# Turning a block's sums: f32 matmuls with the identity instead of f32 transposes

## Chip, cores, metric

The kernel runs on one core of one Trainium2 chip. The metric is the device time of one execution in microseconds (us). TensorE (PE) multiplies, VectorE (DVE), ScalarE (ACT) and GpSimd (POOL) do the elementwise work, and SyncE (SP) issues most of the transfers.

## The reference

The kernel computes the output and the seven gradients of a transformer-like block: attention with 32 heads of 16 columns on a layer-normed input, multiplied by a SiLU gate that an MLP makes of the same input.

```
S, D, H, DH, F = 2048, 512, 32, 16, 1792        # rows, columns, heads, columns of a head, MLP width

xn  = layernorm(x)
s   = attention(xn) @ wo                         # softmax(q k^T / 4) v, per head
g   = silu(gelu(layernorm(xn) @ w1 + b1) @ w2 + b2)
out = x + s * g

out, vjp = jax.vjp(f, x, wqkv, wo, w1, b1, w2, b2)
return out, *vjp(grad_out)
```

All inputs and outputs are bf16. The work that matters here is the core of the attention, which runs the forward and the backward pass together.

## The kernel before

The program has three stages: projections, layer norms and the MLP's first half (`phase_pre`), the attention's core (`attention_core`), and the weights' and the input's gradients (`phase3`). The change lies in the core.

The core works through 64 blocks. Block `j` is a pair of heads (16 pairs) and a quarter of the queries (4 quarters of 512). In a block it goes over 16 groups of 128 keys, `g = 16 j + kb`, for both heads `hj`:

- `s` (line 1532): scores, keys by queries, on PE. `S` (line 1546): their exponential `et`, on ACT.
- `a1` (line 1555): PE multiplies [v, 1, k] by `et` and adds it into rows 0 to 63 of the PSUM bank `X`. After 16 groups these rows hold the block's sums: for each head 16 value sums and the softmax sum (the rest of its 32 rows isn't used).
- `d` (line 1628): PE multiplies the other half of the keys' operand by the tile `dt`. `m` (line 1632): DVE multiplies `d` by `et` into `gts`.
- `a2` (line 1561): PE adds into rows 64 to 127 of `X`; these become the gradient of q. The copy out of it is `dq` (line 1643), on ACT.
- `t` (line 1542) and its exponential (line 1550) make scores the other way round, queries by keys. For two units of a block PE turns `et` instead (`E`, line 1570) and DVE copies the result (`eE`, line 1574). `ze` and `zg` (lines 1663 and 1671) add up the keys' gradients in a bank `Z`; the operand `gk` of `zg` is `gts`, turned by a transfer that SP issues (line 1635). `acc` (lines 1685 and 1687) copies or adds `Z` on DVE.

When a block's 16 groups are in `X`, its sums must be turned, so that queries lie on partitions. This is the chain of the block's end, and the place of the change:

- `xs` (line 1587): DVE copies rows 0 to 63 of `X` to SBUF, 64 x 512, f32.
- `XT` (line 1593): PE turns it in four pieces of 64 x 128 into one PSUM bank, 128 x 4 x 64, f32.
- `xt` (line 1597): DVE copies that bank. `rL` (line 1601): DVE takes the reciprocals of the softmax sums.
- `W` (lines 1610 to 1613): POOL makes the normalized output and the operand `W`.
- `DT` (line 1618) and `dt` (line 1622): PE turns `W`, DVE copies it; `dt` is what the block's `d` matmuls stream.

The tiles `XT`, `DT`, `ET` and `Z` share one PSUM bank (tag `z`), so each waits for the copy of the one before. `d` has one bank for each head, and the scores share two slots of two banks.

The order on every engine is written out ahead: `make_plan` goes through estimated costs, due times (`due`) and free buffers, and `attention_core` emits the steps in that order under a manual schedule. In the estimate `XT` has an entry of its own (line 1199: 400 ns for the group, then a gap of 205). The lag between steps is part of the plan: while one block's sums are turned, PE already works at the scores of the next block and the `d` of this one's predecessor. Matmuls of zeros into `X` (`fill`, lines 1578 and 1580) stand where the plan leaves PE a gap.

One other f32 matmul appears in the argument. Line 451, in `phase_pre`, spreads the heads' largest key norms over all partitions: `ones_h`, 32 x 128, times a diagonal, 32 x 32, both f32.

Of the kernel before, what the change touches and what calls it, by code (L numbers as in the profile page):

```python
# [1452 lines left out]
def attention_core(ctx, tc, opnds, ps_z, tail, NAT_s, NATQ_s, Oall, dQall, dKVT_out, dQT_out, ident_f32, ident_bf, npairs=16, nqc=4):  # L1453

    nc = tc.nc
# [133 lines left out]
    def emit_XT(j):  # L1589
        xs = tiles.pop(("xs", j))  # L1590
        XT = tiles["XT", j] = ps_z.tile([128, 4, 64], f32, name="XT", tag="z")
        for qb in range(4):
            nc.tensor.transpose(XT[:, qb, :], xs[:, qb * 128:(qb + 1) * 128], ident_f32[0:64, 0:64])

    def emit_xt(j):
        xt = tiles["xt", j] = finp.tile([128, 4, 64], f32, name="xt")
# [94 lines left out]
    def emit_sk(p, hj):  # L1691
        ob = tiles["ob", p]
        for x in range(2):
            r0 = p * 64 + hj * 32 + 16 * x
            nc.gpsimd.dma_start(out=dKVT_out[r0:r0 + 16, :], in_=ob[64 * x + 32 * hj:64 * x + 32 * hj + 16, :])

    ET_ = mybir.EngineType
    f = dict(fill=emit_fill, E=emit_E, eE=emit_eE, s=emit_s, t=emit_t, S=emit_exp_s, T=emit_exp_t, a1=emit_a1, a2=emit_a2, xs=emit_xs, XT=emit_XT, xt=emit_xt, rl=emit_rl,
             W=emit_W, DT=emit_DT, dt=emit_dt, d0=lambda g: emit_d(g, 0), d1=lambda g: emit_d(g, 1), m0=lambda g: emit_m(g, 0),
             m1=lambda g: emit_m(g, 1), ze=emit_ze, zg=emit_zg, acc=emit_acc, dq=emit_dq,  # L1700
# [127 lines left out]
```

## Time and profile before

| what | us |
|---|---|
| median of 3 runs | 2188.24 |
| the three runs | 2188.24, 2172.43, 2189.15 |
| the profiled execution | 2197.41 |
| its span, first to last instruction | 2195.6 |

The span is what the trace covers; the profiled execution's own time holds 1.8 us more around it. Its mean granted TensorE clock was 0.976. In the rows of the profile PE stands for matmuls, PEld for loads of the stationary operand (they overlap with PE), and L12 for line 12 of the kernel. A tile's rows are written `out<-in`, with buffer numbers left out; `x4` behind a row of the timeline means that four instructions were merged, and the time in brackets is the engine's idle time before them, with what ended it.

### The profile page before, as it was taken

The page shows a single profiled execution, that of the slowest core. Times are in us where ns is not written, and L with a number is a line of the kernel's source. Part 1 is how long each engine was busy: PE and PEld are TensorE (multiplying, and loading weights), DVE is VectorE, ACT ScalarE, POOL GpSimd, SP SyncE. Part 2 cuts the span into 40 slices and gives each one's busy share as a digit, 9 for nine tenths or more (in the row PEclk, how much of TensorE's full clock was granted, in tenths as well). Part 3 has the DMA queues.
Part 4 walks back from the last instruction along what each step waited for, and adds up shares of the span by engine and source line. Part 5 has one row for each costly group of instructions (what it writes and reads, how often), then busy time and mean ns, then how long its engine had stood idle before and what let it go on. Part 6 is the DMA issues. An engine that isn't in the chain of part 4 may idle for free.

```text
span 2195.6 us, 46078 instructions
## 1 busy us (share of the span) xinstructions
PE 2092.3 (95%) x17683; PEld 749.9 (34%) x17683; DVE 1954.9 (89%) x3485; ACT 1894.6 (86%) x2194; POOL 349.9 (16%) x672
## 2 busy tenths in 40 slices
PE   7999999999999999999999999999999999889999
PEld 3443332333333323323333333233323333334444
DVE  7675999999999999989999999999989997889355
ACT  6667999999999999989999999999989994776233
POOL 4322011111110111111111111120111011520001
PEclk9999999999999999989999999999989998999999
DMA  9884999999999999999999999999999999994971
GB/s 288 273 276 135 226 221 216 228 232 233 226 224 234 222 219 232 230 214 215 234 227 225 229 233 210 229 232 236 227 202 236 221 219 229 264 240 112 181 236 60
DMA packets 1562958, 484.49 MB, mean 221 GB/s; under 512 B 1532432, under 2 KB 1536784, under 8 KB 1562096
## 3 DMA queue, kind: packets, MB, share of 16 engines
q1 hardware_dynamic: 1546256, 441.56, 101.0%
q0 software_dynamic: 12560, 34.74, 6.1%
q10 hardware_dynamic: 3920, 5.24, 0.7%
q8 instruction: 138, 2.26, 0.4%
q14 instruction: 84, 0.69, 0.1%
HBM read 46.52 MB, written 51.12 MB: 44 GB/s over the span
## 4 chain that ended last, share of the span: by engine, by line
PE 64%; DVE 16%; ACT 8%; DMA 7%; issue 3%; SPq 1%; POOL 1%; DVEq 0%; ACTq 0%; POOLq 0%
PE d L1628 13%; PE Z L1663 10%; PE X L1555 9%; DVE gts L1632 8%; PE s L1532 8%; PE t L1542 5%; DMA gk<-gts 4%; ACT e L1550 3%; PE ps_dy L853 2%; PE ps_dhg L787 2%; DVE xs L1587 2%; PE ps_dw L729 2%; DVE eE L1574 2%; ACT et L1546 1%; PE ps_dw L771 1%
## 5 line engine op out<-in xcount | busy, mean ns | idle before, releaser
L1632 DVE TENSOR_TENSOR gts<-d,et 128x512 bf16<-128x512 f32 x1424 | 904.4, 682 | 38.4 <-PE d L1628 19.4
L1546 ACT ACTIVATE et<-s 128x1024 bf16<-128x1024 f32 x712 | 721.6, 1066 | 26.4 <-PE d L1628 15.7
L1628 PE MATMUL d<-dt,KVT 32*128 32x512 bf16 x2048 | 720.7, 388 | 18.3 <-DVE gts L1632 6.4
L1550 ACT ACTIVATE e<-t 128x1024 bf16<-128x1024 f32 x640 | 671.6, 1072 | 29.5 <-PE d L1628 14.8
L1532 PE MATMUL s<-QDT,KVT 32*128 32x512 bf16 x2048 | 403.8, 386 | 23.5 <-ACT e L1550 9.1
L1632 DVE TENSOR_TENSOR gts<-d,dQall 128x512 bf16<-128x512 f32 x624 | 396.7, 682 | 18.3 <-PE d L1628 7.9
L1561 PE MATMUL X<-gts,NAT 128*32 128x512 bf16 x2048 | 407.7, 395 | 0.0
L1671 PE MATMUL Z<-gk,QW 128*32 128x512 bf16 x2048 | 386.1, 396 | 15.8 <-DMA gk<-gts 15.8
L1546 ACT ACTIVATE dQall<-s 128x1024 bf16<-128x1024 f32 x312 | 315.8, 1070 | 11.1 <-PE d L1628 10.1
L1555 PE MATMUL X<-et,NAT 128*32 128x512 bf16 x1424 | 281.4, 392 | 0.8 <-ACT et L1546 0.8
L1542 PE MATMUL t<-KVT,QDT 32*128 32x512 bf16 x1280 | 256.6, 390 | 0.0
L1628 PEld LDWEIGHTS <-KVT 32*128 32x128 bf16 x2048 | 169.1, 91 | 226.8 <-issue 221.7
L1663 PE MATMUL Z<-e,W 128*32 128x512 bf16 x1280 | 243.8, 393 | 0.3 <-DVE xt L1597 0.2
L1532 PEld LDWEIGHTS <-KVT 32*128 32x128 bf16 x2048 | 135.3, 91 | 243.1 <-issue 215.2
L1663 PEld LDWEIGHTS <-W 128*32 128x32 bf16 x2048 | 105.7, 93 | 245.4 <-issue 244.0
L1610 POOL TENSOR_TENSOR On<-xt,rL 128x128 f32<-128x128 f32 x64 | 25.4, 396 | 993.4 <-DVE rL L1601 993.4
L1555 PEld LDWEIGHTS <-NAT 128*32 128x32 bf16 x2048 | 103.0, 95 | 127.1 <-issue 126.9
L1542 PEld LDWEIGHTS <-QDT 32*128 32x128 bf16 x1280 | 82.6, 91 | 140.7 <-issue 128.0
L1555 PE MATMUL X<-dQall,NAT 128*32 128x512 bf16 x624 | 123.6, 392 | 0.0
L1561 PEld LDWEIGHTS <-NAT 128*32 128x32 bf16 x2048 | 100.6, 95 | 63.7 <-issue 57.2
L1663 PE MATMUL Z<-gk,W 128*32 128x512 bf16 x512 | 102.9, 397 | 0.0
L1671 PEld LDWEIGHTS <-QW 128*32 128x32 bf16 x2048 | 89.2, 94 | 25.1 <-DMA gk<-gts 15.5
(223 smaller groups left out, 2621.6 us busy)
## 6 DMA issues: line engine op xcount, KB each, us to landing
gk<-gts SPq DMA_TRANSPOSE x512, 4.5
H1T_s<-h1p SPq DMA_DIRECT2D x28, 256.0 KB, 4.0
dQall<-H1T_s POOLq DMA_DIRECT2D x28, 256.0 KB, 5.0
HGT_s<-hgT SPq DMA_DIRECT2D x21, 256.0 KB, 3.8
NAT_s<-NS SPq DMA_DIRECT2D x4, 1056.0 KB, 5.3
dKVT_s<-ob POOLq DMA_DIRECT2D x64, 64.0 KB, 3.9
gb<-GB_s SPq DMA_DIRECT2D x8, 512.0 KB, 5.9
Rkv<-dKVT_s SPq DMA_DIRECT2D x2, 2048.0 KB, 10.4
```

Of the source, the lines that this page charges most:

```text
L729: nc.tensor.matmul(ps[:], lhsT=hgc[fc // 2][:, t // 4, fc % 2, t % 4, :], rhs=dm_all[:, t, :], start=(t == 0), stop=(t == NT - 1))
L787: nc.tensor.matmul(ps[:], lhsT=w2T[:, dc, fc * 128:(fc + 1) * 128], rhs=dmT[:, dc, ss], start=(dc == 0), stop=(dc == IC - 1))
L1532: nc.tensor.matmul(s[:, hj, :], lhsT=op["KVT"][r, kb * 128:(kb + 1) * 128], rhs=op["QDT"][r, qc * 512:(qc + 1) * 512], start=True, stop=Tr ...
L1542: nc.tensor.matmul(t[:, hj, :], lhsT=op["QDT"][r, q0:q0 + 128], rhs=op["KVT"][r, kc * 512:(kc + 1) * 512], start=True, stop=True, tile_pos ...
L1546: nc.scalar.activation(out=et_of(g)[:, g % 2], in_=tiles.pop(("s", g))[:], func=ACT.Exp)
L1550: nc.scalar.activation(out=e[:], in_=tiles.pop(("t", u))[:], func=ACT.Exp)
L1555: nc.tensor.matmul(X[32 * hj:32 * hj + 32, :], lhsT=op_of(j)["NAT"][:, kb, hj, 0:32], rhs=et_of(g)[:, g % 2, hj], start=(kb == 0), stop=(k ...
L1561: nc.tensor.matmul(X[64 + 32 * hj:96 + 32 * hj, :], lhsT=op_of(j)["NAT"][:, kb, hj, 1:33], rhs=gts_of(g // 2)[:, g % 2, hj], start=(kb == ...
L1628: nc.tensor.matmul(d[:], lhsT=op_of(j)["KVT"][r, kb * 128:(kb + 1) * 128], rhs=tiles["dt", j][r, :], start=True, stop=True, tile_position= ...
L1632: nc.vector.tensor_tensor(out=gts_of(g // 2)[:, g % 2, hj], in0=tiles.pop(("d", g, hj))[:], in1=et_of(g)[:, g % 2, hj], op=ALU.mult)
L1663: nc.tensor.matmul(cur["Z"][32 * hj:32 * hj + 32, :], lhsT=tiles["W", j][:, qb, hj, :], rhs=rhs_of(tiles["e", j, kc], hj, qb) if e is None ...
L1671: nc.tensor.matmul(cur["Z"][64 + 32 * hj:96 + 32 * hj, :], lhsT=QW[p % 2][:, qc * 4 + qb, hj, :], rhs=rhs_of(tiles["g", j, kc], hj, qb), s ...
```

## The change

The four f32 transposes of a block's sums become four matmuls with `xs` as the stationary and the identity as the moving operand. The operands, their shapes, the output and the place in the order are the same.

```
     def emit_XT(j):
         xs = tiles.pop(("xs", j))
         XT = tiles["XT", j] = ps_z.tile([128, 4, 64], f32, name="XT", tag="z")
         for qb in range(4):
-            nc.tensor.transpose(XT[:, qb, :], xs[:, qb * 128:(qb + 1) * 128], ident_f32[0:64, 0:64])
+            nc.tensor.matmul(XT[:, qb, :], lhsT=xs[:, qb * 128:(qb + 1) * 128], rhs=ident_f32[0:64, 0:64], start=True, stop=True)
```

In the built program the two instructions differ in one flag (transpose or not); all five engines issue the same instructions in the same order as before.

More of the change, by code (lines that the diff above doesn't have):

```diff
@@ L1592, in emit_XT @@
         for qb in range(4):
-            nc.tensor.transpose(XT[:, qb, :], xs[:, qb * 128:(qb + 1) * 128], ident_f32[0:64, 0:64])
+            nc.tensor.matmul(XT[:, qb, :], lhsT=xs[:, qb * 128:(qb + 1) * 128], rhs=ident_f32[0:64, 0:64], start=True, stop=True)
     def emit_xt(j):
```

## The prediction

> **What bounds the kernel now.** I read the page's head and its chain first, then the windows of single blocks, then the rows around one turning of the sums, and last the one place where this kernel already does an f32 matmul that is no transpose.
>
> ```profile
> span 2195.6 us, 46078 instructions
> PE 2092.3 (95%) x17683; PEld 749.9 (34%) x17683; DVE 1954.9 (89%) x3485; ACT 1894.6 (86%) x2194; POOL 349.9 (16%) x672
> PE 64%; DVE 16%; ACT 8%; DMA 7%; issue 3%; SPq 1%; POOL 1%; DVEq 0%; ACTq 0%; POOLq 0%
> ```
>
> Three engines are busy for most of the span and the chain changes between them, so shares alone decide nothing. The instructions that change are these (the view of tile XT: count, then min/median/max in ns, first and last start in us; below it, who ended PE's wait before them, us and times):
>
> ```profile
> L1593 PEld LDWEIGHTS XT<-ident_f,xs x256: 133/138/141, 201.3 to 1807.3; 64*128 64x128 f32 x128
> L1593 PE MATMUL XT<-ident_f,xs x256: 221/223/275, 201.3 to 1807.3; 64*128 64x64 f32 x128
>   DVE eE L1574: 17.6, 67
> ```
>
> There are 64 blocks with four transposes each, from 201.3 to 1807.3 us. That is 1606.0 us for 63 steps, 25.49 us each. Four single steps, in the windows view (us; then busy time of PE, PEld, DVE, ACT, POOL; then the granted clock, DMA share, GB/s):
>
> ```profile
> 1018.96:1043.92 24.96, 24.27 (x241) 8.12 (x240) 24.68 (x43) 24.74 (x28) 5.76 (x11) 1.00 1.06 218
> 1143.78:1168.74 24.96, 24.29 (x241) 8.11 (x240) 24.68 (x43) 24.74 (x28) 2.44 (x6) 1.00 1.22 224
> 960.56:993.62 33.06, 29.64 (x241) 8.18 (x240) 25.67 (x43) 25.64 (x28) 3.60 (x8) 0.74 1.18 203
> 1600.15:1631.89 31.74, 29.67 (x241) 8.19 (x240) 25.70 (x43) 25.64 (x28) 2.16 (x5) 0.73 1.26 225
> ```
>
> An undisturbed step takes 24.96 us, twice to the hundredth: a cycle with no loose place, in which DVE is idle for 0.28 us and ACT for 0.22. Disturbed steps make up the rest: 1606.0 - 63 x 24.96 = 33.5 us. In the two that are shown, PE had a quarter less than its full clock. So the question is whether the turning lies on that cycle. One block's rows (start, duration, engine):
>
> ```profile
> 1018.15 2.86 ACT L1546 ACTIVATE et<-s 128x1024 bf16<-128x1024 f32 x3
> 1018.20 0.67 DVE L1574 COPY eE<-ET 128x1024 bf16<-128x1024 bf16 x1
> 1018.80 1.27 DVE L1632 TENSOR_TENSOR gts<-d,et 128x512 bf16<-128x512 f32 x2
> 1018.95 0.32 PEld L1593 LDWEIGHTS XT<-ident_f,xs 64*128 64x128 f32 x4 [0.23 <-DVE eE L1574]
> 1018.96 0.46 PE L1593 MATMUL XT<-ident_f,xs 64*128 64x64 f32 x4
> 1019.34 0.09 PEld L1628 LDWEIGHTS <-KVT 32*128 32x128 bf16 x1
> 1019.53 0.37 PE L1628 MATMUL d<-dt,KVT 32*128 32x512 bf16 x1
> 1019.53 0.39 PE L1532 MATMUL s<-QDT,KVT 32*128 32x512 bf16 x2
> 1020.00 0.40 DVE L1597 COPY xt<-XT 128x256 f32<-128x256 f32 x1
> 1020.33 0.67 DVE L1632 TENSOR_TENSOR gts<-d,et 128x512 bf16<-128x512 f32 x1
> ```
>
> The eE copy ends at 1018.20 + 0.67 = 1018.87 and frees the PSUM bank. XT starts 0.09 later, d and s follow 0.57 after XT's start. The d matmul waits for something else: the first of the two gts products ends at 1018.80 + 0.67 = 1019.47 and d starts 0.06 later. The chain of waits, one block on, goes through the same place:
>
> ```profile
> 1043.24 0.60 DVE eE L1574
> 1043.84 0.61 DVE gts L1632
> 1044.44 0.04 issue
> 1044.49 0.37 PE d L1628
> 1044.86 0.02 PE s L1532 x2
> 1044.88 0.32 PE X L1555 x2
> ...
> 1048.52 0.02 PE d L1628
> 1048.54 0.67 DVE acc L1685
> ```
>
> The rows left out are PE's, without a break. So eE starts both branches: gts and then d, which is on the chain, and XT and then d, which is not. The second is nearly as long. How nearly is told by a block in which XT came late:
>
> ```profile
> 993.62 0.46 PE L1593 MATMUL XT<-ident_f,xs 64*128 64x64 f32 x4
> 994.01 0.09 PEld L1628 LDWEIGHTS <-KVT 32*128 32x128 bf16 x1
> 994.08 0.37 PE L1628 MATMUL d<-dt,KVT 32*128 32x512 bf16 x1
> ```
>
> Here d starts 0.46 us after XT's start. So the four transposes have 0.57 - 0.46 = 0.11 us to spare in an ordinary block, and whatever they take beyond that moves d, and with it the s matmuls and all that PE issues after them.
>
> **The change part by part.** It swaps 256 f32 transposes for 256 f32 matmuls of the same operands (xs stationary, the identity moving). Nothing is reordered, no wait is added or taken away, no tile changes, the plan's own estimate of the step stays. The consumers (xt, rL, the POOL products, DT) are the same. What is open is the price of the instruction, and the kernel has it once: line 451 multiplies f32 ones by an f32 diagonal, in one call. Line 451 in the source view, then in the timeline with the weight load that follows:
>
> ```profile
> L451 PEld LDWEIGHTS ps_kb<-kmd,ones_h x2: 181/182/184, 75.0 to 75.1; 32*128 32x128 f32 x2
> L451 PE MATMUL ps_kb<-kmd,ones_h x2: 271/282/293, 75.0 to 75.1; 32*128 32x32 f32 x2
> 75.00 0.29 PEld L451 LDWEIGHTS ps_kb<-kmd,ones_h 32*128 32x128 f32 x2 [0.42 <-issue]
> 75.00 0.40 PE L451 MATMUL ps_kb<-kmd,ones_h 32*128 32x32 f32 x2
> 75.33 0.76 PEld L269 LDWEIGHTS <-w_sb 128*128 128x128 bf16 x5
> ```
>
> One call left two weight loads and two matmuls, where a transpose leaves one pair (256 of each for 64 x 4). I therefore expect 512 pairs at line 1593, eight per block. The distance between loads, with 128 columns loaded in both cases: for the transposes (0.32 - 0.14) / 3 = 0.06 us; at line 451, 0.29 - 0.18 = 0.11 us. The next load follows 75.33 - 75.11 = 0.22 after line 451's last one, and 1019.34 - 1019.13 = 0.21 after the transposes' last.
>
> The first d after the new group then can start, counted from the first load, after 7 x 0.11 + 0.22 + 0.07 = 1.06 us (0.07 from d's load to d, in the block with the late XT). Today it starts at 0.57. So d is late by 0.49 us per block. The bounds of the distance: not below 0.06, the transposes' own, which gives 7 x 0.06 + 0.29 = 0.71 and 0.14 us per block; 0.13 by the matmuls of line 451 instead of its loads (0.40 less 0.27 for one of them), 1.20 and 0.63 us; and 0.18, one load's whole duration, if nothing overlaps, 1.55 and 0.98 us. I take 0.11, since the row is of the same load, and line 451 streams 32 columns where XT streams 64, which could only push it up. A gain from the instruction itself is excluded: each has the same operands, and no row of an f32 matmul is shorter than the transposes.
>
> [...] The row: twice the pairs, 0.11 / 0.06 = 1.8 times as far apart, 3.7 times together. [...]
>
> What hides it? XT's consumers first. XT now ends at 1018.96 + 0.46 = 1019.42 and xt starts at 1020.00, so 0.58 us of its growth is covered; the new end, about 7 x 0.11 + 0.05 + 0.28 = 1.10 after the start, or 1020.06, costs the copy some 0.1 us. For the d branch there is no cover but the 0.11 us already counted. The d that is 0.49 later ends at 1019.90 + 0.49 = 1020.39, and the gts that takes it started at 1020.33, so DVE goes idle. The s beside it, ready at 1019.53 + 0.39 = 1019.92, feeds the third of the three activations that run back to back from 1018.15 to 1021.01, so ACT goes idle too. Both have only the 0.28 and 0.22 us per step that they idle today, and these lie at other places.
>
> The sum: 63 steps x 0.49 = 31 us. Against the profiled execution, 2197.4 us (its span 2195.6 and 1.8 us around it), that makes 2228 us. The median of the runs shown is 2188.2, so there 2219 us, 1.4% more. With the bounds: 63 x 0.14 = 9 us, 63 x 0.63 = 40 us, 63 x 0.98 = 62 us.
>
> **The rivals.** *The pairs cost more.* The distance is 0.13 or above, since 64 columns are streamed instead of 32, or a load has to wait for the matmul before it. For it: both durations at line 451 are longer than the transposes' (182 against 138 ns, 282 against 223). Against it: the second load there began 0.11 after the first, before the first matmul's 0.28 were over. 2188 + 40 = 2228 to 2250. Chance 0.20.
>
> *Slack elsewhere takes half of it.* The late d is made up for later in the step, at a place where PE waits for ACT or DVE. For it: DVE and ACT are 24.7 of 24.96 busy, not all of it. Against it: the chain after d runs PE row after PE row for the next 4 us. 2188 + 15 = 2203. Chance 0.11.
>
> *The change doesn't do what it says*: the identity matmul is built as one pair, or as two at the old distance. Then d is late by at most 0.14 us, 2188 to 2197. Line 451's two records speak against it. Chance 0.06.
>
> *Not slower, by the transfers.* The 33.5 us of disturbed steps begin where Z waits for a gk that a transfer has to turn:
>
> ```profile
> PE Z L1671 <- DMA gk<-gts: 14.2, 10, 2.9
> PEld L1671 <- DMA gk<-gts: 13.3, 9, 3.3
> ```
>
> These are the two rows of that wait in the view of waits over 201 to 1807 us: some ten times, up to 3.3 us. In the two steps shown the granted clock was 0.74 and 0.73, so a wait of 3 us costs 7 to 8 in all. A step that is 2% longer gives the same ten turnings 2% more time; if SP's queue then catches up, the waits and the slow stretches go. The point at which it decides: all 31 us of the sum have to be found in the 33.5, that is, nearly every disturbed step must vanish, 2186 us; 9 us found is enough for a result within 1%. Against it: the turnings start from products that are late by the same 0.49 us, and the quiet steps have no wait to lose. Chance 0.11, of it 0.03 that it comes together with cheap pairs, 2188 + 9 - 33 = 2164.
>
> **How the numbers follow.** About 1%, 22 us, is what a measurement of this kernel can tell from no change: 2166 to 2210. My forecast has the chance 0.52: 2219 us, by itself 2210 to 2230. Slower by over 1%: 0.52 + 0.20 = 0.72. Within 1%: 0.11 + 0.06 + 0.08 = 0.25. Faster: 0.03. The range goes down to 2196, where the half-absorbed case and the upper part of the cheap pairs are still held, and up to 2240, into the dearer pairs; outside are the 0.11 of the transfers, some 0.02 of the cheap pairs and 0.05 above.
>
> **What would show it.** In the profile after: 512 loads and 512 matmuls at line 1593, and 256 more PE instructions on the page; loads 0.11 apart (a group of about 0.95 us instead of 0.32); the first d 1.06 us after the group's start, no longer released by gts; quiet steps of 25.45 us instead of 24.96, clock 1.00. The prediction is wrong if the loads stay 256, if quiet steps stay under 25.2 us with eight pairs in them, or if the disturbed steps change by more than 10 us.

## The result and the profile after

| what | before | after |
|---|---|---|
| median of 21 runs each, us | 2178.2 (2170.74 to 2189.15) | 2193.59 (2186.67 to 2210.14) |
| ratio, 95% interval | | 1.0066 [1.0051, 1.0082] |
| the profiled execution, us | 2197.41 | 2186.67 |
| its span, us | 2195.6 | 2184.9 |

The kernel became slower by 15.4 us, 0.7%: within the 1% that the prediction took for no change, though the interval is clear of 1. The two profiled executions stand the other way round. The one of before is slower than any of these 21, the one of after is as fast as the fastest of its own. So the two traces may be compared step by step, but not by their totals.

The head of the page of after, the granted clock in 40 slices of the span, and the chain of waits by engine:

```profile
span 2184.9 us, 46546 instructions
PE 2095.1 (96%) x17895; PEld 787.0 (36%) x17939; DVE 1962.8 (90%) x3485; ACT 1891.0 (87%) x2194; POOL 349.1 (16%) x672
PEclk9999999999999999999999999999999998999999
PE 53%; ACT 24%; DVE 13%; issue 6%; DMA 3%; POOL 1%; SPq 0%; DVEq 0%; ACTq 0%; POOLq 0%
```

PEld has exactly 256 instructions more than before (17939 - 17683); PE has 212 more on record, since some matmul records are missing. The clock row of before is:

```profile
PEclk9999999999999999989999999999989998999999
```

Slices 18 and 30, in the core, are under nine tenths there and full now. The 8 in slice 34 is in both; that slice begins behind the core's last block.

The turning in the view of tile XT (count, then min/median/max in ns, first and last start in us), and the copy that precedes it, 64 times, in the view of tile xs:

```profile
L1593 PEld LDWEIGHTS XT<-ident_f,xs x512: 182/188/188, 201.7 to 1802.8; 64*128 64x128 f32 x171
L1593 PE MATMUL XT<-ident_f,xs x512: 272/272/320, 201.7 to 1802.8; 64*128 64x64 f32 x171
L1587 DVE COPY xs<-X x64: 670/672/683, 200.0 to 1800.6; 64x512 f32<-64x512 f32 x64
```

512 pairs, as forecast. The 63 steps of the core, taken from the first xs to the last, last 1600.6 us, against 1606.0 before. Two single steps in the windows view (us; busy time of PE, PEld, DVE, ACT, POOL; granted clock; DMA share; GB/s):

```profile
962.36:987.79 25.43, 24.71 (x245) 8.68 (x243) 24.86 (x43) 24.75 (x28) 3.62 (x8) 1.00 1.22 228
1573.05:1598.48 25.43, 24.71 (x246) 8.68 (x244) 24.86 (x43) 24.75 (x28) 3.61 (x8) 1.00 1.22 228
```

The undisturbed step went from 24.96 to 25.43 us. Over 63 steps that is 29.4 us (with the medians of the trace unrounded, 0.466 us each). But in this trace nearly every step is such a step (the longest takes 26.23 us): 1600.6 - 63 x 25.43 = -1.5 us, where 33 us stood before. (It can be below zero because the first step is some 3.3 us shorter than the others, in every run.) The timeline of one block's end (start, duration, engine):

```profile
961.61 0.67 DVE L1574 COPY eE<-ET 128x1024 bf16<-128x1024 bf16 x1
962.21 1.27 DVE L1632 TENSOR_TENSOR gts<-d,et 128x512 bf16<-128x512 f32 x2
962.36 0.96 PEld L1593 LDWEIGHTS XT<-ident_f,xs 64*128 64x128 f32 x8 [0.23 <-DVE eE L1574]
963.39 0.09 PEld L1628 LDWEIGHTS <-KVT 32*128 32x128 bf16 x1
963.39 0.39 PE L1628 MATMUL d<-dt,KVT 32*128 32x512 bf16 x1
963.57 0.42 DVE L1597 COPY xt<-XT 128x256 f32<-128x256 f32 x1
963.91 0.68 DVE L1632 TENSOR_TENSOR gts<-d,et 128x512 bf16<-128x512 f32 x1
```

Eight loads take 0.96 us, so they are (0.96 - 0.18) / 7 = 0.11 us apart. d starts 963.39 - 962.36 = 1.03 us after the group's start, where it was 0.57. The chain of waits passes through the turning now:

```profile
962.11 0.32 PE X L1555 x2
962.43 1.03 PE XT L1593 x8
963.46 0.32 PE d L1628
963.78 0.06 PE s L1532 x2
963.84 0.02 issue
963.86 0.78 ACT et L1546
```

Before, eE, gts and d stood at this place. So the per-block cost is what it was said to be. What is missing is the other thing that the trace of before had: Z's waits for a gk. In the view of waits over 201 to 1807 us one row of it is left (us in all, times, longest):

```profile
PEld L1671 <- DMA gk<-gts: 0.2, 1, 0.2
```

Before it was 14.2 us at PE and 13.3 at PEld, in about ten places. What such a wait did can be read in the PE rows of a disturbed step of before:

```profile
972.59 0.39 PE L1663 MATMUL Z<-e,W 128*32 128x512 bf16 x2
975.91 0.61 PE L1671 MATMUL Z<-gk,QW 128*32 128x512 bf16 x2 [2.93 <-DMA gk<-gts]
976.45 0.61 PE L1532 MATMUL s<-QDT,KVT 32*128 32x512 bf16 x2
```

PE idles for 2.93 us and then runs at half pace, 0.61 us where 0.39 is usual. In the core of before the records of the granted clock show six stretches at half, 54.6 us together. Five of them, 51.2 us, begin within 3 us of the end of such a wait; the first, 3.4 us at 224.9, follows none. In the core of after there is no stretch at half.

### The profile page after: what moved, and what is told of

Same layout as the page of the kernel before. It is cut to its first block, busy times and chain, and to the rows that moved or that the text cites. A ratio compares the mean times of both kernels' runs of the same rounds, so it can differ in the third digit from the quotient of the medians.

```text
span 2184.9 us, 46546 instructions
## 1 busy us (share of the span) xinstructions
PE 2095.1 (96%) x17895; PEld 787.0 (36%) x17939; DVE 1962.8 (90%) x3485; ACT 1891.0 (87%) x2194; POOL 349.1 (16%) x672
## 4 chain that ended last, share of the span: by engine, by line
PE 53%; ACT 24%; DVE 13%; issue 6%; DMA 3%; POOL 1%; SPq 0%; DVEq 0%; ACTq 0%; POOLq 0%
ACT e L1550 13%; PE d L1628 10%; PE s L1532 9%; PE X L1555 7%; ACT et L1546 7%; DVE gts L1632 6%; PE Z L1663 6%; PE t L1542 3%; PE XT L1593 3%; ACT dQall L1546 2%; PE ps_dy L853 2%; PE ps_dhg L787 2%; ACT cq L1643 2%; PE ps_dw L771 1%; PE X L1561 1%
## 5 line engine op out<-in xcount | busy, mean ns | idle before, releaser
L1628 PE MATMUL d<-dt,KVT 32*128 32x512 bf16 x2048 | 704.8, 381 | 19.0 <-DVE gts L1632 18.6
L1532 PE MATMUL s<-QDT,KVT 32*128 32x512 bf16 x2048 | 398.4, 381 | 20.1 <-ACT e L1550 10.9
L1561 PE MATMUL X<-gts,NAT 128*32 128x512 bf16 x2048 | 400.2, 388 | 0.0
L1671 PE MATMUL Z<-gk,QW 128*32 128x512 bf16 x2048 | 379.6, 389 | 1.5 <-DMA gk<-gts 1.5
L1542 PE MATMUL t<-KVT,QDT 32*128 32x512 bf16 x1280 | 250.1, 382 | 0.0
L1610 POOL TENSOR_TENSOR On<-xt,rL 128x128 f32<-128x128 f32 x64 | 25.4, 396 | 1010.9 <-DVE rL L1601 1010.9
L1574 DVE COPY eE<-ET 128x1024 bf16<-128x1024 bf16 x128 | 86.5, 676 | 5.2 <-PE ET L1570 5.1
```

The source lines that it names most:

```text
L1532: nc.tensor.matmul(s[:, hj, :], lhsT=op["KVT"][r, kb * 128:(kb + 1) * 128], rhs=op["QDT"][r, qc * 512:(qc + 1) * 512], start=True, stop=Tr ...
L1542: nc.tensor.matmul(t[:, hj, :], lhsT=op["QDT"][r, q0:q0 + 128], rhs=op["KVT"][r, kc * 512:(kc + 1) * 512], start=True, stop=True, tile_pos ...
L1561: nc.tensor.matmul(X[64 + 32 * hj:96 + 32 * hj, :], lhsT=op_of(j)["NAT"][:, kb, hj, 1:33], rhs=gts_of(g // 2)[:, g % 2, hj], start=(kb == ...
L1574: nc.vector.tensor_copy(out=eE[:], in_=tiles.pop(("ET", u))[:])
L1628: nc.tensor.matmul(d[:], lhsT=op_of(j)["KVT"][r, kb * 128:(kb + 1) * 128], rhs=tiles["dt", j][r, :], start=True, stop=True, tile_position= ...
L1671: nc.tensor.matmul(cur["Z"][64 + 32 * hj:96 + 32 * hj, :], lhsT=QW[p % 2][:, qc * 4 + qb, hj, :], rhs=rhs_of(tiles["g", j, kc], hj, qb), s ...
```

## The experiments

Three theories were set against each other at first.

1. **The queue.** The steps cost 29.4 us. In SP's queue the turnings run one after another (640 at line 1635 in the trace of before, none begun ahead of the end of the one before it). The longer step gives it more time, so gk is late more rarely, and part of the cost comes back as waits and half-clock stretches that no longer happen.
2. **The kind of instruction.** A guess that the two profiles allow: the f32 matmuls keep the clock up where the transposes do not (54.6 us of the core at half before, none after); the longer step is not the reason.
3. **Chance.** Executions vary by some 20 us; the profile of before was a bad one, that of after a good one, and the steps cost only half of what one trace shows.

All runs first, so that each can be read against the others. "Step" is the median step between two xs copies of the one profiled execution; "excess" is what its 63 steps took beyond 63 such steps; "waits" is Z's waiting for gk as the view of waits gives it, at PEld and at PE; "half clock" is the time in the core with the clock granted at one half.

| run | median us (runs) | ratio to before [95%] | step | excess | waits | half clock |
|---|---|---|---|---|---|---|
| before | 2178.2 (21) | | 24.96 | 33.3 | 13.3, 14.2 | 54.6 |
| after | 2193.59 (21) | 1.0066 [1.0051, 1.0082] | 25.43 | -1.5 | 0.2, 0 | 0 |
| e1 transposes, three times | 2186.29 (12) | 1.0035 [1.0002, 1.0068] | 25.28 | 4.9 | 4.1, 4.1 | 0 |
| e2 two of four are matmuls | 2181.69 (12) | 1.0004 [0.9979, 1.0029] | 25.11 | 20.2 | 12.8, 8.6 | 34.1 |
| e3 the matmuls twice | 2310.7 (6) | 1.06 [1.0561, 1.0638] | 26.32, 28.29 | | none | 204.8 |
| e4 plan: later landing | 2180.92 (12) | 0.9997 [0.9964, 1.0029] | 24.96 | 22.4 | 13.7, 11.6 | 27.3 |
| e5 before, other transfers spread | 2192.59 (12) | 1.0045 [1.0014, 1.0075] | 24.96 | 34.0 | 16.5, 13.2 | 64.9 |
| e6 after, other transfers spread | 2192.72 (12) | 1.007 [1.004, 1.0101] | 25.43 | 6.1 | 3.6, 1.9 | 17.1 |
| e7 transposes, seven times | 2240.85 (4) | 1.0281 [1.0237, 1.0324] | 26.27 | 1.0 | none | 6.8 |
| e8 six matmuls | 2292.89 (1) | | 27.30 | | none | 160.4 |
| e9 before, a turning less | 2161.73 (12) | 0.9928 [0.9902, 0.9954] | 24.96 | -0.3 | none | 3.4 |
| e10 after, a turning less | 2190.63 (12) | 1.0066 [1.0032, 1.01] | 25.43 | -1.5 | none | 0 |

Each ratio is against runs of before made beside it, whose medians were 2178.2 to 2180.5 us.

### e1: the longer step without a matmul

```diff
-        for qb in range(4):
+        for qb in [0, 1, 2, 3] * 3:
             nc.tensor.transpose(XT[:, qb, :], xs[:, qb * 128:(qb + 1) * 128], ident_f32[0:64, 0:64])
```

> Each block's four transposes are issued three times over (12 pairs instead of 4, the last four count; the output is unchanged), no matmul with the identity. Pairs 0.062 us apart: the first d is about 0.36 us later than before, quiet steps 25.32 us instead of 24.96, which by itself costs 63 x 0.36 = 23 us. Theory 1 (a longer step gives the transfers that turn gk time to catch up, whatever makes it longer): waits of Z for gk under 5 us in all, no slow stretch of the clock in the core, 2157 + 23 = 2180 to 2188 us. Theory 2 (real matmuls keep the clock up where transposes do not): waits and slow stretches as before the change, 2178 + 23 = 2201 us. Theory 3 (chance, the waits come and go from run to run whatever the kernel): also about 2201 us.

Twelve transposes per block, no matmul. The step grew to 25.28 us, by 0.32 of the matmuls' 0.47. The waits of e1, over its core (us, times, longest):

```profile
PEld L1671 <- DMA gk<-gts: 4.1, 8, 0.9
PE Z L1671 <- DMA gk<-gts: 4.1, 6, 1.8
```

They shrank from 3.3 us at the longest to 1.8, and no half-clock stretch followed any of them. The steps alone would cost 20 us (63 x 0.32); the median rose by 6.8 (2186.29 against 2179.5; 0.4 to 14.8 by the ratio's interval). So part of the cost comes back without any matmul, and theory 2, which put 2201 here, falls. That the queue gave it back is not shown by this run: see the table in the section on e9.

### e2: half of the change

```diff
-            nc.tensor.transpose(XT[:, qb, :], xs[:, qb * 128:(qb + 1) * 128], ident_f32[0:64, 0:64])
+            if qb < 2:
+                nc.tensor.transpose(XT[:, qb, :], xs[:, qb * 128:(qb + 1) * 128], ident_f32[0:64, 0:64])
+            else:
+                nc.tensor.matmul(XT[:, qb, :], lhsT=xs[:, qb * 128:(qb + 1) * 128], rhs=ident_f32[0:64, 0:64], start=True, stop=True)
```

> Two of a block's four pieces stay transposes, two become matmuls. Six pairs; the first d is about 0.15 us later than before, quiet steps 25.11 us, by itself 9 us. Theory 1: the waits for gk shrink in part, somewhere between before and after: 2175 to 2185 us. Theory 2: with half the matmuls the waits' slow stretches are already rarer, 2157 + 9 + up to 10 = 2166 to 2176 us. Theory 3: waits as before, 2178 + 9 = 2187 us.

Two pieces by transposes, two by matmuls, six pairs in all. The waits of e2 (its Z line is 1674):

```profile
PEld L1674 <- DMA gk<-gts: 12.8, 12, 3.0
PE Z L1674 <- DMA gk<-gts: 8.6, 5, 2.6
```

The step grew by 0.15 us, 9.3 us over 63; the median grew by 2.2. In this one profile the waits are nearly those of before, at PE 8.6 us instead of 14.2. Here the ratio's interval includes 1, so the run alone decides nothing. It is the lowest point of a row: growth by the steps 9, 20 and 29 us in e2, e1 and after, growth of the median 2.2, 6.8 and 15.4. What comes back is 7, 13 and 14 us, each uncertain by 3 to 7 us by the ratios' intervals.

### e3: the matmuls twice

```diff
-        for qb in range(4):
-            nc.tensor.transpose(XT[:, qb, :], xs[:, qb * 128:(qb + 1) * 128], ident_f32[0:64, 0:64])
+        for qb in [0, 1, 2, 3] * 2:
+            nc.tensor.matmul(XT[:, qb, :], lhsT=xs[:, qb * 128:(qb + 1) * 128], rhs=ident_f32[0:64, 0:64], start=True, stop=True)
```

> The four matmuls with the identity are issued twice over (16 pairs of 0.112 us; the output is unchanged). The first d is 0.89 us later than in the changed kernel, quiet steps 26.32 us. Theory 1 and 2: no waits for gk are left, the whole growth is passed on: 2187 + 56 = 2243 to 2250 us. Theory 3: 2178 + 63 x 1.36 = 2264 us. If slack elsewhere in the step could take up part of a late d, quiet steps would be under 26.2 us.

Sixteen pairs per block, expected as a step that is simply longer. It was that, and something else on top: 2310.7 us lies above all the numbers expected. Two neighbouring steps of e3 in the windows view:

```profile
990.52:1018.81 28.29, 27.98 (x254) 9.39 (x252) 25.13 (x43) 25.26 (x28) 2.44 (x6) 0.88 1.10 216
1018.81:1045.13 26.32, 25.60 (x254) 9.57 (x252) 24.87 (x43) 24.74 (x28) 3.60 (x8) 1.00 1.19 222
```

The second is the step by its instructions: 26.32 us, the sixteen pairs at 0.11 us each. The first is 1.97 us longer and has a clock of 0.88. The core lasts 1718.9 us, 60.7 more than 63 steps of 26.32, which is about what 2310.7 lies above theory 1's 2243 to 2250. A block of that kind in the timeline of e3:

```profile
881.31 1.86 PEld L1593 LDWEIGHTS XT<-ident_f,xs 64*128 64x128 f32 x16 [0.23 <-DVE eE L1574]
883.24 0.60 PE L1628 MATMUL d<-dt,KVT 32*128 32x512 bf16 x1
```

The d behind the group takes 0.60 us instead of 0.39, and PE has waited for nothing but eE, 0.23 us. So no wait for a gk opened this stretch, and none is on record in e3's core. What stands right before it is the group of f32 matmuls. In after, with eight pairs, there is no such stretch. That speaks against theory 2 a second time, and e7 and e8 follow it up.

### e4: a later landing in the plan

```diff
-           half_end=410, copy=618, copy_end=768, rl=115, pool=430, sp=2100, land=3700, sp_wait=120, map_wait=120)
+           half_end=410, copy=618, copy_end=768, rl=115, pool=430, sp=2100, land=4700, sp_wait=120, map_wait=120)
```

> The kernel before, with transposes, but the plan assumes that a turned gk lands 4.7 instead of 3.7 us after its issue, so it orders the Z matmuls somewhat later against the rest. If late landings against a plan that counts on 3.7 us are the cause of the disturbed steps (what theory 1 rests on), the waits for gk fall to under 10 us with quiet steps still near 24.96 us: 2157 to 2170 us, faster than before. If the slow stretches come from PE's activity (theory 2) or by chance (theory 3), nothing changes: 2175 to 2180 us. The reordered plan can itself cost up to 0.3 us per step (19 us).

The transposes of before are kept; the plan is told that a turned gk lands 1 us later than it assumed. The order hardly changes by it: of the plan's 13644 steps 395 stand in another place, and the time that the plan leaves from the issue of a turning to the first Z matmul that uses it is 9.79 us in the mean with both values. So the edit does not order Z later, as it was meant to. The waits of e4:

```profile
PEld L1671 <- DMA gk<-gts: 13.7, 12, 3.3
PE Z L1671 <- DMA gk<-gts: 11.6, 11, 2.9
```

They are as they were (13.3 and 14.2 before), and so is the time, 0.9997 [0.9964, 1.0029]. Theory 1's 2157 to 2170 us did not come, but the run doesn't test it either. What it gives is a second profile of almost the same order: its excess is 22.4 us and its half clock 27.3, against 33.3 and 54.6, so single profiles differ by that much.

### e5 and e6: the other transfers, spread out

```diff
-            ff=360, ffd=300, fe=360, fed=150, eo0=-3, eo1=-4, ntk=8, ntq=16, pqq=2, pqd=20, pna=27, pnb=32, psq=26, psk=40, psk2=60, xs_act=0, dq_act=1,
+            ff=360, ffd=300, fe=360, fed=150, eo0=-3, eo1=-4, ntk=8, ntq=16, pqq=6, pqd=20, pna=27, pnb=32, psq=36, psk=40, psk2=60, xs_act=0, dq_act=1,
```

> The kernel before, with transposes, but POOL's own transfers no longer go out in bunches: the load of NATQq no longer follows the second dKVT store at once, and the two dQT stores go out after the NAT loads instead of right before them. Same work, quiet steps as before, 24.96 us. Theory 1, now with its first cause (a turning of gk that meets a bunch of POOL's transfers lands late, the plan of the short step has no room for it, Z waits and the clock drops): landings over 7.5 us and waits of Z for gk all but vanish, 2157 to 2168 us, faster than before by 0.5 to 1%. Theory 2 (real matmuls keep the clock up) and theory 3 (chance): 2175 to 2182 us.

> The same spreading in the changed kernel, quiet steps 25.43 us. Theory 1: the few waits that the changed kernel has left go too, 2183 to 2190 us; against the transposes with the same spreading it is slower by the full 63 x 0.466 = 29 us, 1.3 to 1.4%, which is what the prediction said of the change by itself. Theories 2 and 3: 2190 to 2196 us, and the difference to the transposes stays near 15 us.

What first makes a turning late? In before, the turnings that meet one of POOL's own transfers are slower: 243 of the 656 in the core took 2.48 us to issue and 5.29 to land in the mean, the other 413 took 2.12 and 4.56. So POOL's transfers were moved apart, in before (e5) and in after (e6). The slowest landings went: over 7.5 us there were 11 before and 2 in e5. But more turnings met a POOL transfer, 300 instead of 243, and the waits of e5 did not shrink:

```profile
PEld L1671 <- DMA gk<-gts: 16.5, 14, 2.9
PE Z L1671 <- DMA gk<-gts: 13.2, 9, 2.5
```

The time rose where it was expected to fall, 1.0045 [1.0014, 1.0075]. That a few slow landings behind bunched transfers are the first cause falls with this. The pair tells something else, though. e5 and e6 differ by the change alone, and their medians are 2192.59 and 2192.72 us, of 12 runs each (the ratios' intervals, 1.0014 to 1.0075 and 1.004 to 1.0101, overlap). The step of e6 is the 25.43 us of after, 29.4 us more over 63; and its waits are

```profile
PEld L1671 <- DMA gk<-gts: 3.6, 4, 1.8
PE Z L1671 <- DMA gk<-gts: 1.9, 2, 1.4
```

a fifth of e5's. So the 29 us that theory 1 expected between the two did not show: where more is lost to late turnings to start with, the change cost nothing that can be seen (0.1 us, with some 7 us of uncertainty from 12 runs each).

### e7 and e8: which instruction pulls the clock down

```diff
# e7
-        for qb in range(4):
+        for qb in [0, 1, 2, 3] * 7:
             nc.tensor.transpose(XT[:, qb, :], xs[:, qb * 128:(qb + 1) * 128], ident_f32[0:64, 0:64])
# e8
-        for qb in range(4):
-            nc.tensor.transpose(XT[:, qb, :], xs[:, qb * 128:(qb + 1) * 128], ident_f32[0:64, 0:64])
+        for qb in [0, 1, 0, 1, 2, 3]:
+            nc.tensor.matmul(XT[:, qb, :], lhsT=xs[:, qb * 128:(qb + 1) * 128], rhs=ident_f32[0:64, 0:64], start=True, stop=True)
```

> The four transposes issued seven times over (28 pairs, the last four count), about as long a group as that of the matmuls twice (1.66 against 1.67 us from first to last load), no matmul with the identity. Quiet steps 26.3 us. If f32 matmuls are what drops the clock (there it fell to half for 6.8 us in every other step), there is no slow stretch here: 2160 + 63 x 1.35 = 2245 us. If any such group does (a stretch in which little of the array is used), the clock falls here too: about 2310 us.

> Six matmuls with the identity instead of four (12 pairs; the output is unchanged). Quiet steps 25.43 + 0.45 = 25.87 us. Without slow stretches of the clock 2187 + 28 = 2215 us; if the clock already falls now and then, 2220 to 2260 us.

28 transposes, or twelve matmul pairs, per block. A step of e7 in the windows view, and the end of its group in the timeline:

```profile
988.25:1014.52 26.27, 25.55 (x265) 9.51 (x264) 24.86 (x43) 24.74 (x28) 3.62 (x8) 1.00 1.24 222
```

```profile
988.25 1.94 PE L1593 MATMUL XT<-ident_f,xs 64*128 64x64 f32 x28
990.12 0.39 PE L1628 MATMUL d<-dt,KVT 32*128 32x512 bf16 x1
```

A step of e8 in the windows view, and PE's rows inside it:

```profile
1001.47:1028.78 27.31, 26.46 (x249) 8.90 (x247) 24.99 (x43) 24.96 (x28) 3.60 (x8) 0.94 1.11 215
```

```profile
1001.47 1.55 PE L1593 MATMUL XT<-ident_f,xs 64*128 64x64 f32 x12
1002.96 0.38 PE L1628 MATMUL d<-dt,KVT 32*128 32x512 bf16 x1
...
1003.61 0.60 PE L1628 MATMUL d<-dt,KVT 32*128 32x512 bf16 x1
...
1007.11 0.39 PE L1663 MATMUL Z<-e,W 128*32 128x512 bf16 x2
```

The group of 28 transposes takes 1.94 us, longer than the 1.55 of twelve matmul pairs and nearly the 2.00 of e3's sixteen; its step is 26.27 us, the clock stays at 1.00, and the d behind it takes 0.39 us. The step of e8 without a half-clock stretch is 25.88 us, as forecast; most of its steps are 27.31, with a clock of 0.94. The matmuls in it take 0.38 us, then 0.60 from 1003.61 on, then 0.39 again by 1007.11: a stretch of about 3.4 us. The records show 45 such stretches in e8's core of 63 steps, one of 10.2 us and the others of 3.4, 160.4 us in all. (Its time, 2292.89 us, is a single run and above the 2260 expected; the argument rests on its trace.) So theory 2 has it the wrong way round: where there were more f32 matmuls the clock did not hold better but fell, to half for 160.4 us of e8's core with 12 pairs and for 204.8 of e3's with 16, where after's 8 pairs left none; behind the 28 transposes of e7, nearly as long a group as e3's, it fell once (6.8 us, in the second step, where before has a stretch of 3.4 too).

e7 also tests theory 1 from the other end. With no waits for gk left, all of the steps' growth should show: 63 x (26.27 - 24.96) = 82.5 us. The median grew by 60.3 (2240.85 against 2180.53), so 22 us came back, with the ratio's interval 12 to 31, the most of any run; the interval includes the 16.7 us that e9 below finds there is to win back.

### e9 and e10: relieve the queue, not the step

```diff
     def emit_map(k, src, j, kc, h):
+        if k == "e" and h == 1:
+            return
...
-    def rhs_of(m, hj, qb):
-        return m[:].rearrange("q a (r h b) k -> q a r h b k", r=2, h=2)[:, :, :, hj, qb, :]
+    def rhs_of(m, hj, qb, one=False):
+        v = m[:].rearrange("q a (r h b) k -> q a r h b k", r=2, h=2)[:, :, :, hj, qb, :]
+        return v[:, 0:1].to_broadcast([128, 2, 2, 128]) if one else v
...
-                             rhs=rhs_of(tiles["e", j, kc], hj, qb) if e is None else e[:, hj, :],
+                             rhs=rhs_of(tiles["e", j, kc], hj, qb, True) if e is None else e[:, hj, :],
```

> The kernel before, with transposes, but SP leaves out one of a block's ten turnings (the second half of the map of e; Z reads the first half twice, so those keys' gradients aren't the reference's). PE, DVE, ACT and POOL issue the same instructions in the same order; quiet steps 24.96 us. Spreading POOL's transfers did not help, so theory 1 now rests on the queue alone: SP's turnings take some 2.25 us each, 22.5 to 27 us of a step of 25, and any slow one leaves a backlog that a short step cannot work off. It expects that with a tenth of the turnings gone Z's waits for gk and the clock's slow stretches vanish at the short step too: core 63 x 24.96 = 1573 us instead of about 1600, 2155 to 2165 us in all. If the waits have another cause than the queue's load (chance, the clock, single slow landings): 2172 to 2182 us.

> The same with the matmuls with the identity (the same keys' gradients aren't the reference's). Quiet steps 25.43 us, no waits. Theory 1: slower than the same kernel with transposes by the full 63 x 0.466 = 29 us, 2184 to 2192 us. If the matmuls' cost were really only half of that, as the measured 15 us of the change says, the two would be 13 to 17 us apart.

This is the direct test. About one turning in ten leaves SP's queue (594 of 656 between the first xs and the last remain), in before (e9) and in after (e10); PE's work and its order stay, though Z reads one half of that map twice and the keys' gradients are not the reference's. The turnings of gts in the view of the line that issues them (min/median/max ns of one in SP's queue), of before:

```profile
L1635 SPq DMA_TRANSPOSE gk<-gts x512: 1316/2068/6154, 209.3 to 1848.8; - x171
```

And of e9:

```profile
L1637 SPq DMA_TRANSPOSE gk<-gts x512: 1315/1870/3767, 209.1 to 1809.3; - x171
```

With the means of all turnings in the core, the queue of before is occupied for 656 x 2.25 / 63 = 23.5 us per step of 24.96, that is 94%; that of after for 656 x 2.18 / 63 = 22.7 of 25.43, 89%; that of e9 for 594 x 2.03 / 63 = 19.1 of 24.96, 77%. Steps of e9:

```profile
923.88:948.84 24.96, 24.28 (x242) 8.09 (x240) 24.68 (x43) 24.74 (x28) 2.43 (x6) 1.00 1.06 215
1573.20:1598.16 24.96, 24.28 (x241) 8.10 (x240) 24.67 (x43) 24.74 (x28) 2.16 (x5) 1.00 0.95 202
```

The quiet step is that of before to the hundredth, no row of Z waiting for gk is left, and the excess is -0.3 us. The median fell by 16.7 us (2178.47 to 2161.73; 0.9928 [0.9902, 0.9954]). So 16.7 us is what the late gks cost before, in the median of its runs (10 to 21 by the interval). And with them out of the way the change costs its full price: e10 - e9 = 2190.63 - 2161.73 = 28.9 us (some 4 us uncertain), beside the 29.4 that the steps give. Taking the turning out of after, which has next to no such waits, moves nothing that can be measured (1.0066 to before with it, 1.0066 without).

The traces also show how far behind the queue is, when the rows of the products, the turnings and Z are matched by the plan's order. "Behind" is the time from the end of a turning's last product on DVE to its start on SP, the mean and the longest of the 500 turnings of gts in the core. "Margin" is the median time from the landing of a pair of turnings to the first weight load of Z that uses it; "on arrival" counts the pairs that were used within 0.1 us of landing.

| run | step, us | behind, us | margin, us | on arrival |
|---|---|---|---|---|
| before | 24.96 | 2.97 (10.23) | 4.01 | 15 of 250 |
| e1 | 25.28 | 3.16 (8.99) | 3.89 | 14 of 250 |
| e6 | 25.43 | 2.42 (7.40) | 4.56 | 4 of 250 |
| after | 25.43 | 1.76 (7.03) | 5.50 | 1 of 250 |
| e7 | 26.27 | 1.53 (7.00) | 6.23 | 0 of 250 |
| e9 | 24.96 | 0.50 (3.54) | 6.19 | 0 of 179 |

(For e9 the landing of both turnings is known for 179 pairs.) In after, the queue is 1.2 us less behind than before, the margin is 1.5 us wider, and all but one pair land ahead of their use; taking a turning out does the same at the short step. e1 does not fit: with 0.32 us more per step its queue is as far behind as before, and only its waits are shorter. Why its median stays 13 us under the cost of its steps is open.

Theory 1 holds for after, e6 and e7, and theory 3 falls: the cost of the steps is there in full in the medians once the waits are out, and the relief is there in the medians of e6 and e7 as well. What e9 does not separate is SP's queue from the DMA engines that it feeds: fewer turnings also made each one shorter, 2.03 us in the mean instead of 2.25. A part of chance stays in the single profiles: the excess of before's, 33 us, is twice the 16.7 us of the medians, as its total, above all 21 of the runs, also tells.

## Why the prediction was right or wrong

**The instruction.** Two pairs per f32 matmul, 512 in all, 0.11 us apart: as line 451 had shown. The distance was the same with 64 columns streamed here as with 32 there, and the rival *the pairs cost more* is out with it.

**The place on the path.** Right. d at 1.06 us after the group's start was forecast, 1.03 measured; a quiet step of 25.45, 25.43 measured; 31 us for 63 steps, 29.4 from the trace and 28.9 between e9 and e10. No slack elsewhere took any of it, so *slack elsewhere takes half of it* is out, though its number, 2203, lies closer to the result than the forecast does.

**What was left unchanged in the sum.** Here it failed. The sum added 31 us and took the 33.5 us of disturbed steps into the new time as they were. They did not stay: from 33.3 to -1.5 us in the two profiles, and by about 14 us in the medians (29.4 - 15.4). This was the mechanism of the rival *not slower, by the transfers*, with a chance of 0.11, and it acted, though it took half of the cost and not all. The reason given against it was "the turnings start from products that are late by the same 0.49 us, and the quiet steps have no wait to lose". The first half is true and beside the point: the products come later, but so do all deadlines, and a queue that was occupied for 94% of a step gets 0.47 us more in which to work off what an earlier slow turning had put back: it was 2.97 us behind in the mean before and 1.76 after. The second half is true of the quiet steps; it is in the others that the waits arise. The price of a wait was misread on the way: "a wait of 3 us costs 7 to 8" fits the step at 960.56, but in the one at 1600.15 PE waited 1.59 us and the step lost 31.74 - 24.96 = 6.8. The text did put down as a sign of error that "the disturbed steps change by more than 10 us". That sign showed.

**The base.** The number forecast was 2219 us, 25.4 above the result. 10.0 of that is the base, 2188.24 as the median of three runs where 21 runs have 2178.2; 14.0 is the relief; 1.4 is the step's size (30.8 added, 29.4 measured). As a change, 1.4% was said and 0.66% [0.51, 0.82] came. So *slower by over 1%* was wrong, and *within 1%*, at 0.25, right; the median lies 2.4 us below the range. With 2178.2 as the base the same sum would have given 2209 and the range would have held the result; that would have been luck, since the relief would have been missing from it all the same.

**What could not be settled.** Why a turning slips in the first place in before was not found. Of its 15 pairs that were used on arrival, four landed 8.0 to 11.1 us after their issue and most of the others had started 4 to 9 us behind their products; the spread of POOL's transfers (e5) did not move the waits, and the plan's landing time (e4) hardly moved the order. Runs of after up to 2210 us are unexplained too, since only its fastest has a trace. A kernel that keeps the transposes and has no such waits would be the gain; e9 shows what it is worth, 16.7 us, but leaves out work. Whether another buffer for the turned gk could give it without that was not tried.

## What to carry to other kernels

Where steps of a pipeline are disturbed now and then, ask what each disturbance is fed by before carrying its cost through a sum: here a transfer queue that was occupied for 94% of a step was a second bottleneck, and a step that got 0.47 us longer on the first one earned half of its cost back there. The test is cheap: take one transfer out of the queue and look at the quiet step and the total separately. And the profile of an execution that is slower than the timed runs shows the disturbances at their worst; take the step's price from it, but the price of the disturbances from medians.

## What the runs showed of the hardware

An f32 matmul left two pairs of load and matmul in the records (512 for the 256 at line 1593 of after, two for the one at line 451), loads 0.11 us apart against 0.06 for an f32 transpose of the same piece: a group of four takes 0.96 us of loads instead of 0.32.

Not expected was the clock. Behind a group of f32 matmuls with the identity the granted clock fell to half although PE had waited there for nothing but eE (0.23 us ahead of the group shown of e3, 15.8 us in 65 such waits in e8): not once with 8 pairs (0.96 us, after and e10), for 3.4 us in most steps with 12 pairs (e8), for 6.8 us in every other step with 16 (1.86 us, e3), and with 28 f32 transposes only once, in the second step (6.8 us at 225.4, e7). That one is not e7's own: before, with four transposes, e4 and e9 have a stretch of 3.4 to 10.2 us at the same place, 224.7 to 225.0, and so has e6 (3.4 us at 223.6); the other stretch in e6 that lies inside the core began behind a wait for gk. In e8 PE was busy for 26.46 of the 27.31 us of such a step, in e3 for 27.98 of 28.29. What the granted clock goes by is not shown: in e3 and e8 against e7 it was the f32 matmuls behind which it fell and the f32 transposes behind which, but for the second step, it did not.
